# Pooled attention and two feed-forward layers on one core: attention and weight preparation moved to the one-product steps, squares on ScalarE, pools in the other order, 96 bytes added

## The chip, the cores and the metric

The kernel runs on one core of a Trainium2 chip. The metric is the time of one execution on the device in microseconds (us); the median of three runs of the kernel before is 1854.59 us.

## The reference

Three layers follow one another, all in float32:

```python
# 1: attention, B, H, S, D = 8, 8, 576, 64; keys and values averaged over groups of 8
k_p = k.reshape(B, H, 72, 8, D).mean(axis=3); v_p = v.reshape(B, H, 72, 8, D).mean(axis=3)
scores = np.matmul(q, k_p.transpose(0, 1, 3, 2)) / 8
attn = softmax(scores); x = np.matmul(attn, v_p)      # laid out as 4608 tokens x 512
# 2: 512 -> 2048 -> 512
h = x @ w_in; g = s * np.maximum(h, 0)**2 + b; x = g @ w_out
# 3: 512 -> 1536 -> 512
out = (sigmoid(x @ w_gate) * (x @ w_val)) @ w_out2
```

## The kernel before

Every operand of the large products is split into a high and a low part in the type float32r, and a product is three matmuls (low x high, high x high, high x low). Weights arrive as 64-bit words; `convert` makes float32 of them (one ScalarE and three VectorE instructions a tile) and `split` makes the two parts (ScalarE copies the high part, VectorE or GpSimd subtracts).

**First part** (layers 1 and 2). The tokens are 9 blocks of 512. A list of 176 slots sets the order: 16 slots for block 0, then for each of four pairs of blocks (p = 0 to 3) 40 slots x = 0 to 39. In a slot x < 32 the first product of layer 2 for one group of 128 hidden rows runs (`emit_h`, 12 matmuls of 512 columns; those of the next pair's x = 0 and 1 are put at x = 32 and 33 of this pair). Two slots later the second product of a chunk runs (`mm_chunk`). A pair's second product goes by a scheme with fewer multiplications: eight steps for each of z = 0 to 4. Steps with x < 24 (z = 0, 1, 2) have one product of 6 matmuls, steps of z = 3 and z = 4 two of them, 12 matmuls. So a one-product step holds 18 matmuls, a step of z = 3 has 24, a step of z = 4 has 12 and no `emit_h`. From slot 16 on TensorE's order is the order in which the program is written; the other engines' orders and the DMA queue of SyncE (SP) are set by a planner that simulates the program when it is built.

Beside the slots, at half-slot positions (`events`), runs the attention of layer 1: 18 units of 256 tokens (`scores`, `norm`, `left`, `turn`, `values`), units 0 and 1 ahead of the slots. A unit takes 13 positions, that is 6.5 slots. Keys and values of a batch are loaded up to 20 positions ahead and summed by GpSimd (`pool_k`, `pool_v`). `starts` holds the units' first positions: 0, 16, 32, 48, 64, 80 for units 2 to 7, then 80 p + 16, 40, 64, 80. A slot x of pair p is position 32 + 80 p + 2 x, so in p = 0 units start at x = 0, 8, 16, 24 and 32, in p = 1 and 2 at x = 4, 16, 24 and 32, and in p = 3 at x = 4.

`prep_w2` prepares layer 3's weights in 12 x 9 parts, one a slot, in slots 34 to 141. `prep_s` (layer 2's combined weights) stands at slots 14 to 45. `gen_x` prepares layer 3's first inputs `xo` beside slots 155 and 159.

**Second part** (layer 3). For each of four pairs and 12 groups `first_half` and `second_half` run seven `product`s of six matmuls (weights `w7` stationary, `xo` moving), `emit_o` the output product; the last block has 12 groups of four `product`s. 2,304 matmuls are `product`'s. `w1_stack.close()` ends the first part's pools, and `w7p`, `wo2p`, `g2p` and `wk` take their place; a tile of theirs waits for the tiles of the first part that lay there.

**Where the tiles lie.** Pools on the left side are stacked upwards in the order of their definition: constants, `gp`, `cvp`, then `w1_stack`: `wr_p` (12 KB a partition), `gs_p` (34), `us_p` (8), `gr_p` (2), `rawp` (12), `wi_p` (12), `xp` (32). `w7p` (two tiles of 14 KB) therefore lies on `wr_p` and eight tiles of `gs_p`. Attention's pools lie on the right side, and later `xop` with `xo`. In the allocation of the program before, every left tile that TensorE reads in the second part begins at a multiple of 256 bytes, `xo` begins at 172,000, which is 224 above a multiple of 256, 96 above a multiple of 128 and 32 above a multiple of 64; attention's operands `v1h`, `v1l`, `v3`, `t1` to `t3` on the right have the same remainders as `xo`. Between the last byte of the left side and the first of the right side 96 bytes are free in the first part.

Of the kernel before, what the change touches and what calls it, by code (L numbers as in the profile page):

```python
# [8 lines left out]
F32 = mybir.dt.float32  # L9
F32R = mybir.dt.float32r  # L10
I32 = mybir.dt.int32
ACTF = mybir.ActivationFunctionType
ALU = mybir.AluOpType
# [6 lines left out]
def pooled_attention_two_ffn(ctx, tc, q, k, v, v_left, w_in, w_out, s_in, b_in, w_gate, w_val, w_out2, out):  # L20
# [8 lines left out]
    nc = tc.nc  # L29
    NT, DM = out.shape  # L30
    NU, _, NP, UNIT = q.shape
# [3 lines left out]
    H = 2 * NP  # L35
    KD = DM // 128
    M1 = w_in.shape[0]
    M2 = w_gate.shape[0]
    NB = NT // 512

    const = ctx.enter_context(tc.tile_pool(name="const", bufs=1))
# [7 lines left out]
    ident = const.tile([128, 128], F32, name="ident")  # L49
    s_sb = const.tile([128, 1], F32, name="s_sb")  # L50
    b_sb = const.tile([128, 1], F32, name="b_sb")

    def split(hi, lo, src, eng):

        nc.scalar.activation(out=hi, in_=src, func=ACTF.Copy)  # L55
        eng.tensor_tensor(out=lo, in0=src, in1=hi.bitcast(F32), op=ALU.subtract)  # L56
# [3 lines left out]
    NB1 = NBLK // 2  # L60
    H1 = M1 // 2
# [7 lines left out]
    def load64(src):  # L69
        raw = rawp.tile([128, 1024], I32, tag="raw", name="raw")  # L70
        nc.sync.dma_start(out=raw, in_=src.bitcast(I32))
        return raw

    def cv_tile():
        return cvp.tile([128, 512], I32, tag="cv", name="cv")
# [19 lines left out]


    w1_stack = ExitStack()
    wr_p = w1_stack.enter_context(tc.tile_pool(name="wr_p", bufs=3))
    gs_p = w1_stack.enter_context(tc.tile_pool(name="gs_p", bufs=17))
    us_p = w1_stack.enter_context(tc.tile_pool(name="us_p", bufs=1))  # L100
    gr_p = w1_stack.enter_context(tc.tile_pool(name="gr_p", bufs=1))
    rawp = w1_stack.enter_context(tc.tile_pool(name="rawp", bufs=3))
    wi_p = w1_stack.enter_context(tc.tile_pool(name="wi_p", bufs=3))
    xp = w1_stack.enter_context(tc.tile_pool(name="xp", bufs=2))
    at_stack = ExitStack()
    at1 = at_stack.enter_context(tc.tile_pool(name="at1", bufs=1, side="right"))
    at2 = at_stack.enter_context(tc.tile_pool(name="at2", bufs=2, side="right"))
# [53 lines left out]
    def gs_tile():  # L161
        return gs_p.tile([128, 512], F32, tag="gs", name="gs")
# [56 lines left out]
    def store_split(dst, raw, src):  # L219
        n = src.shape[1]  # L220
        t = raw.rearrange("p (two f) -> p two f", two=2)[:, :, :n]
        split(t[:, 0].bitcast(F32R), t[:, 1].bitcast(F32R), src, nc.gpsimd)
        later.append((dst, t))

    def raw_tile():
        return rawp.tile([128, 1024], I32, tag="raw", name="raw")

    def prep_w2(m, part):
        h0, h1 = slice(0, 256), slice(256, 512)
        if part == 0:  # L230
            prep["g"] = load64(w_gate[m])
        elif part == 1:
            prep["v"] = load64(w_val[m])
        elif part == 2:
            raw = prep["g"]
            prep["gt"] = convert(raw, cv_tile())
            store_split(w7d[m][:, :, 256:768], raw, prep["gt"])
        elif part == 3:
            prep["vt"] = convert(prep["v"], cv_tile())
            store_split(w7d[m][:, :, 0:256], raw_tile(), prep["vt"][:, h0])  # L240
        elif part == 4:
            gt, vt, c = prep["gt"], prep["vt"], cv_tile().bitcast(F32)
            for o, a, b_, op in ((c[:, h1], gt[:, h0], vt[:, h0], ALU.subtract), (vt[:, h0], vt[:, h0], vt[:, h1], ALU.add),
                                 (c[:, h0], vt[:, h0], gt[:, h0], ALU.subtract), (gt[:, h1], gt[:, h1], c[:, h0], ALU.subtract)):
                nc.gpsimd.tensor_tensor(out=o, in0=a, in1=b_, op=op)
            prep["c"] = c
        elif part == 5:
            store_split(w7d[m][:, :, 768:1280], prep["v"], prep["vt"])
        elif part == 6:
            store_split(w7d[m][:, :, 1280:1792], raw_tile(), prep["c"])  # L250
        elif part == 7:
            store_split(w7d[m][:, :, 1792:2048], raw_tile(), prep["gt"][:, h1])
            prep["o"] = load64(w_out2[m])
        else:
            store_split(wo2d[m], prep["o"], convert(prep["o"], cv_tile()))
# [3 lines left out]
    def emit_h(i):  # L259
        j, m = steps[i]  # L260
        n = blocks[j][1]
        hi, lo = wi.pop(i)
        ps = ps_b.tile([128, 512], F32, tag="b", name="hps")[:, :n]
        a, c = x_tiles(j)
        step = UNIT if i < 2 else n
        for t0 in range(0, n, step):
            f = slice(t0, t0 + step)
            for kk in range(KD):
                nc.tensor.matmul(out=ps[:, f], lhsT=hi[:, kk], rhs=c[:, kk, f], start=kk == 0, stop=False)  # L269
                nc.tensor.matmul(out=ps[:, f], lhsT=hi[:, kk], rhs=a[:, kk, f], start=False, stop=False)  # L270
                nc.tensor.matmul(out=ps[:, f], lhsT=lo[:, kk], rhs=a[:, kk, f], start=False, stop=kk == KD - 1)  # L271
        first = j % 2
        if j and m < H1:
            g = gs_tile()
        else:
            g = gp.tile([128, 512], F32, tag="g", name="g", bufs=3)
        nc.scalar.activation(out=g, in_=ps, func=ACTF.Relu)
        if first:
            nc.vector.tensor_tensor(out=g, in0=g, in1=g, op=ALU.mult)
        else:  # L280
            nc.scalar.activation(out=g, in_=g, func=ACTF.Square)
        if j == 0:
            nc.scalar.activation(out=g, in_=g, func=ACTF.Identity, scale=s_sb, bias=b_sb)
        g_t[j, m] = g
# [304 lines left out]
    def left(u, t):  # L589
        pm, pl = e_t[u, t]  # L590
        lt = at2.tile([128, H, 4, 8], F32R, tag="lt", name="lt")
        for sl in (0, 2):
            nc.scalar.activation(out=lt[:, :, sl], in_=pl, func=ACTF.Copy)
        for sl in (1, 3):
            nc.vector.tensor_tensor(out=lt[:, :, sl], in0=pl, in1=lt[:, :, sl - 1].bitcast(F32), op=ALU.subtract)
        e_t[u, t] = pm, lt

    def turn(u, t, part):
# [44 lines left out]
    def at(pos, fn, *args):  # L643
        events.setdefault(pos, []).append((fn, args))

    starts = [16 * (u - 2) for u in range(2, 8)]
    for p in range(1, NB1):
        starts += [80 * p + x for x in (16, 40, 64, 80)]
    starts = dict(enumerate(starts, 2))
    for b in range(1, B):  # L650
        p = starts[b * S // UNIT]
        at(max(p - 20, 0), load_kv, b, "k")
# [8 lines left out]
    for u in range(2, NU):  # L661
        p = starts[u] + (2 if u == 2 else 0)
# [70 lines left out]
    if True:  # L733
# [61 lines left out]
        chunks = [(None, i) for i in range(M1)] + [(p, x) for p in range(NB1) for x in range(5 * H1)]  # L795
        hidden, used = {}, []
        for slot, (p, x) in enumerate(chunks):
# [4 lines left out]
            if p is None or x >= 3 * H1 or x % 2:  # L802
                used.append((slot + LAG, p, x))
        asked = M1

        def mm(slot):
            p, x = chunks[slot]
# [6 lines left out]
        for slot, (p, x) in enumerate(chunks):  # L814
            i = hidden.get(slot)
            swap = p is not None and x == 4 * H1 + 1
            if slot == M1:
                pe_order.enter_context(tc.manual_schedule(engines={mybir.EngineType.PE}))
            store_later()
            for fn, args in events.pop(2 * slot, []):  # L820
                fn(*args)
            if i is not None:
                load_wi(i + 3)
                if not swap:
                    emit_h(i)
            if 34 <= slot < 34 + 9 * M2:
                prep_w2(*divmod(slot - 34, 9))
            if M1 - 2 <= slot < 2 * M1 - 2:
                prep_s(*divmod(slot - M1 + 2, 2))
            if slot == 2 * M1:  # L830
                prep_bias()
            if p is None:
                split_wi(i + 2)
                split_g(i)
                split_wo(i + 1)
                load_wo(i + 2)
            else:
                prep_chunk(p, x, 0)
            for fn, args in events.pop(2 * slot + 1, []):
                fn(*args)  # L840
            if slot >= LAG:
                mm(slot - LAG)
            if p is not None:
                prep_chunk(p, x, 1)
            if swap and i is not None:
                emit_h(i)
            while asked < len(used) and used[asked - 3][0] <= slot:
                _, p1, x1 = used[asked]
                fetch_s(p1, x1 - (x1 < 3 * H1))
                asked += 1  # L850
            if p is not None and 3 * H1 - 2 <= x < 4 * H1 - 2:
                reload(p, x - 3 * H1 + 2)
            if i == NS - M1:
                assert not any(y < 2 * len(chunks) for y in events), events
                at_stack.close()
                xop = ctx.enter_context(tc.tile_pool(name="xop", bufs=1, side="right", reuse_waits="tile"))
            if i in (NS - M1 + 3, NS - M1 + 7):
                gen_x(0, (i - NS + M1) // 7)
# [180 lines left out]
```

## Time and profile before

| | |
|---|---|
| median of three runs | 1854.59 us (1852.23 to 1854.65) |
| the profiled execution | 1852.05 us, its span 1850.3 us |
| busy share of the span | TensorE 94%, VectorE 61%, ScalarE 39%, GpSimd 24% |
| mean granted TensorE clock | 0.969 of full speed |
| ahead of block 0's first `emit_x` matmul | 0 to 81.2 us |
| block 0 | 81.2 to 207.5 us |
| pairs p = 0 to 3 | 207.5 to 1011.0 us |
| second part | 1011.0 to 1850.3 us |

The span is that of the profiled execution, 1.75 us shorter than its time. Busy times of engines overlap. A stage of the first part is given by the first matmuls of its `mm_chunk`s: pairs p = 0 to 3 begin at 207.5, 431.7, 637.4 and 839.6 us, their z = 3 at 338.1, 545.6, 751.9 and 943.8, their z = 4 at 389.5, 598.4, 803.9 and 979.2. PEclk is the share of full speed that TensorE was granted, 1 for 2.4 GHz and 0.5 for 1.2 GHz at any moment.

### The profile page before, as it was taken

To read this page: it belongs to the slowest core of one execution; us is meant where nothing else is said; L and a number is where in the kernel's file an instruction comes from. 1 tells how busy PE (TensorE), PEld (TensorE's weight loads), DVE (VectorE), ACT (ScalarE), POOL (GpSimd) and SP (SyncE) were. 2 spreads that over 40 slices of the span, in tenths; PEclk is the share of its full clock that TensorE was granted. 3 is DMA by queue.
4 is the path that set the end of the run, shared out by engine and by line. 5 is a ranking of instruction groups with operands and counts; after the bars stand their busy time and mean duration, and the time that the engine had idled before them with its cause. 6 is when DMAs were issued, how large, how long until landed. Compare 5 with 4: busy or idle time off the path is not lost.

```text
span 1850.3 us, 22182 instructions
## 1 busy us (share of the span) xinstructions
PE 1736.1 (94%) x7848; PEld 1422.2 (77%) x7848; DVE 1124.4 (61%) x1736; ACT 721.1 (39%) x1303; POOL 436.0 (24%) x447
## 2 busy tenths in 40 slices
PE   4688899979999899989997999999999999999999
PEld 4566687768877788778886888888888888888887
DVE  7999766878678786875474544554445544454111
ACT  2556545545555555554454222222222222222111
POOL 5788605444252363321000000000000000000000
PEclk7788999989999899999998999999999999999999
DMA  7667998969897889867877555855585558554764
GB/s 273 237 196 243 350 315 267 324 238 329 302 329 271 253 332 351 304 222 235 257 221 256 184 172 200 284 188 183 187 284 190 198 173 286 194 193 169 264 228 141
DMA packets 159550, 454.46 MB, mean 246 GB/s; under 512 B 15696, under 2 KB 37200, under 8 KB 159440
## 3 DMA queue, kind: packets, MB, share of 16 engines
q1 hardware_dynamic: 155920, 441.51, 69.4%
q0 software_dynamic: 3520, 11.54, 1.9%
q8 instruction: 62, 1.02, 0.2%
q14 instruction: 48, 0.39, 0.1%
HBM read 371.20 MB, written 81.79 MB: 245 GB/s over the span
## 4 chain that ended last, share of the span: by engine, by line
PE 68%; DVE 13%; DMA 7%; POOL 4%; issue 4%; ACT 2%; SPq 0%; POOLq 0%; ACTq 0%; DVEq 0%
PE pc L887 5%; PE pc L885 5%; PE pc L886 5%; PE acc L942 5%; PE acc L941 5%; PE acc L943 5%; PE pb L885 4%; PE pb L886 4%; PE pb L887 4%; PE hps L269 4%; PE hps L271 4%; PE hps L270 4%; PE acc L374 3%; PE acc L376 3%; PE acc L375 3%
## 5 line engine op out<-in xcount | busy, mean ns | idle before, releaser
L891 DVE TENSOR_TENSOR wk<-pc,wk 128x512 f32<-128x512 f32 x192 | 132.5, 690 | 249.5 <-PE pc L887 247.6
L269 PE MATMUL hps<-xl,wi 128*128 128x512 f32 (+1 forms) x584 | 238.3, 408 | 13.0 <-DVE xl L56 5.8
L271 PE MATMUL hps<-xh,wi 128*128 128x512 f32 (+1 forms) x584 | 233.1, 399 | 0.0
L270 PE MATMUL hps<-xh,wi 128*128 128x512 f32 (+1 forms) x584 | 232.0, 397 | 0.0
L753 POOL DMA_DIRECT2D cv<-x2d x36 | 19.5, 542 | 712.1 <-DMA out<-eo 621.2
L374 PE MATMUL acc<-gl,wr 128*128 128x512 f32 x448 | 179.3, 400 | 2.6 <-DVE gl L56 2.1
L375 PE MATMUL acc<-gh,wr 128*128 128x512 f32 x448 | 177.0, 395 | 0.0
L376 PE MATMUL acc<-gh,wr 128*128 128x512 f32 x448 | 176.9, 395 | 0.0
L902 ACT ACTIVATE g<-pb 128x512 f32<-128x512 f32 x60 | 35.9, 598 | 361.9 <-PE pb L887 361.9
L886 PE MATMUL pc<-xo,w 128*128 128x512 f32 x432 | 170.9, 396 | 0.0
L887 PE MATMUL pc<-xo,w 128*128 128x512 f32 x432 | 170.9, 396 | 0.0
L885 PE MATMUL pc<-xo,w 128*128 128x512 f32 x432 | 170.9, 395 | 0.0
L55 ACT ACTIVATE gh<-g 128x512 fp32r<-128x512 f32 x140 | 87.8, 627 | 168.2 <-DVE g L903 144.3
L56 DVE TENSOR_TENSOR gl<-gs,gh 128x512 fp32r<-128x512 f32 x160 | 125.7, 790 | 32.4 <-ACT gh L55 30.1
L885 PE MATMUL pb<-xo,w 128*128 128x512 f32 x336 | 133.9, 398 | 9.3 <-DMA w<-w7d 9.3
L269 PEld LDWEIGHTS hps<-xl,wi 128*128 128x128 f32 x584 | 114.0, 195 | 35.9 <-DVE xl L56 6.0
L55 ACT ACTIVATE gh<-gs 128x512 fp32r<-128x512 f32 x160 | 100.3, 629 | 88.7 <-DVE gs L300 41.0
L886 PE MATMUL pb<-xo,w 128*128 128x512 f32 x336 | 133.6, 398 | 0.0
L887 PE MATMUL pb<-xo,w 128*128 128x512 f32 x336 | 133.4, 397 | 0.0
L271 PEld LDWEIGHTS hps<-xh,wi 128*128 128x128 f32 x584 | 114.2, 196 | 24.2
L270 PEld LDWEIGHTS hps<-xh,wi 128*128 128x128 f32 x584 | 114.1, 195 | 21.4
L56 POOL TENSOR_TENSOR raw<-cv,raw 128x512 fp32r<-128x512 f32 (+1 forms) x72 | 95.6, 1334 | 147.1 <-ACT raw L55 128.7
(143 smaller groups left out, 3713.3 us busy)
## 6 DMA issues: line engine op xcount, KB each, us to landing
w<-w7d SPq DMA_DIRECT2D x48, 1792.0 KB, 7.6
wi<-w1d SPq DMA_DIRECT2D x128, 512.0 KB, 5.3
wr<-s1d SPq DMA_DIRECT2D x224, 256.0 KB, 4.5
wo<-wo2d SPq DMA_DIRECT2D x108, 512.0 KB, 4.5
raw<-in SPq DMA_DIRECT2D x68, 512.0 KB, 5.5
w7d<-raw SPq DMA_DIRECT2D x36, 512.0 KB, 4.3
w<-w7d SPq DMA_DIRECT2D x12, 1280.0 KB, 6.5
kv<-in SPq DMA_DIRECT2D x24, 512.0 KB, 6.4
```

The source lines that it names most:

```text
L55: nc.scalar.activation(out=hi, in_=src, func=ACTF.Copy)
L56: eng.tensor_tensor(out=lo, in0=src, in1=hi.bitcast(F32), op=ALU.subtract)
L269: nc.tensor.matmul(out=ps[:, f], lhsT=hi[:, kk], rhs=c[:, kk, f], start=kk == 0, stop=False)
L270: nc.tensor.matmul(out=ps[:, f], lhsT=hi[:, kk], rhs=a[:, kk, f], start=False, stop=False)
L271: nc.tensor.matmul(out=ps[:, f], lhsT=lo[:, kk], rhs=a[:, kk, f], start=False, stop=kk == KD - 1)
L374: nc.tensor.matmul(out=a, lhsT=w[:, 0, f], rhs=gl, start=begin, stop=False, skip_group_check=True)
L375: nc.tensor.matmul(out=a, lhsT=w[:, 0, f], rhs=gh, start=False, stop=False, skip_group_check=True)
L376: nc.tensor.matmul(out=a, lhsT=w[:, 1, f], rhs=gh, start=False, stop=end, skip_group_check=True)
L885: nc.tensor.matmul(out=ps, lhsT=w[:, 0, x, kk], rhs=r[:, 1, kk, :n], start=first and kk == 0, stop=False, skip_group_check=True)
L886: nc.tensor.matmul(out=ps, lhsT=w[:, 0, x, kk], rhs=r[:, 0, kk, :n], start=False, stop=False, skip_group_check=True)
L887: nc.tensor.matmul(out=ps, lhsT=w[:, 1, x, kk], rhs=r[:, 0, kk, :n], start=False, stop=kk == 1, skip_group_check=True)
L891: nc.vector.tensor_tensor(out=o, in0=ps, in1=b_, op=ALU.add)
```

## The change

- `starts`: units 2 and 3 stay at 0 and 16; the others start at x = 0, 6, 12 and 18 of each pair, so that they lie in slots x < 24.5.
- `prep_w2`: its 108 parts go to the slots from 34 on with x < 32 (without every fourth of p = 1's z = 3), the last one being slot 167. None stands beside z = 4.
- `emit_h`: the square of blocks 1, 3, 5 and 7 (64 instructions) is made by ScalarE instead of VectorE.
- `left`: two ScalarE and two VectorE instructions of 64 elements become one and one of 128.
- `w1_stack`: its pools are defined in the other order, `xp` first and `wr_p` last, so that `w7p` and `wo2p` lie on `xp` and `wi_p`.
- A constant of 96 bytes a partition is added, which nothing reads. All pools on the left side behind it move by 96 bytes.

```diff
+    const.tile([128, 24], F32, name="pad")
...
-    wr_p = w1_stack.enter_context(tc.tile_pool(name="wr_p", bufs=3))
-    gs_p = w1_stack.enter_context(tc.tile_pool(name="gs_p", bufs=17))
+    xp = w1_stack.enter_context(tc.tile_pool(name="xp", bufs=2))
+    wi_p = w1_stack.enter_context(tc.tile_pool(name="wi_p", bufs=3))
+    rawp = w1_stack.enter_context(tc.tile_pool(name="rawp", bufs=3))
     us_p = w1_stack.enter_context(tc.tile_pool(name="us_p", bufs=1))
     gr_p = w1_stack.enter_context(tc.tile_pool(name="gr_p", bufs=1))
-    rawp = w1_stack.enter_context(tc.tile_pool(name="rawp", bufs=3))
-    wi_p = w1_stack.enter_context(tc.tile_pool(name="wi_p", bufs=3))
-    xp = w1_stack.enter_context(tc.tile_pool(name="xp", bufs=2))
+    gs_p = w1_stack.enter_context(tc.tile_pool(name="gs_p", bufs=17))
+    wr_p = w1_stack.enter_context(tc.tile_pool(name="wr_p", bufs=3))
...
-        if first:
-            nc.vector.tensor_tensor(out=g, in0=g, in1=g, op=ALU.mult)
-        else:
-            nc.scalar.activation(out=g, in_=g, func=ACTF.Square)
+        nc.scalar.activation(out=g, in_=g, func=ACTF.Square)
...
-        for sl in (0, 2):
-            nc.scalar.activation(out=lt[:, :, sl], in_=pl, func=ACTF.Copy)
-        for sl in (1, 3):
-            nc.vector.tensor_tensor(out=lt[:, :, sl], in0=pl, in1=lt[:, :, sl - 1].bitcast(F32), op=ALU.subtract)
+        l4 = lt.rearrange("p h (c two) j -> p h c two j", two=2)
+        both = pl.unsqueeze(2).to_broadcast([128, H, 2, 8])
+        nc.scalar.activation(out=l4[:, :, :, 0], in_=both, func=ACTF.Copy)
+        nc.vector.tensor_tensor(out=l4[:, :, :, 1], in0=both, in1=l4[:, :, :, 0].bitcast(F32), op=ALU.subtract)
...
-    starts = [16 * (u - 2) for u in range(2, 8)]
-    for p in range(1, NB1):
-        starts += [80 * p + x for x in (16, 40, 64, 80)]
-    starts = dict(enumerate(starts, 2))
+    starts = [0, 16] + [2 * M1 + 80 * p + x for p in range(NB1) for x in (0, 12, 24, 36)]
+    starts = dict(enumerate(starts[:NU - 2], 2))
...
+        light = [slot for slot, (p, x) in enumerate(chunks) if slot >= 2 * M1 + 2 and x < 4 * H1 and (x < 3 * H1 or x % 4 or p != 1)]
+        parts = dict(zip(light, (divmod(i, 9) for i in range(9 * M2))))
...
-            if 34 <= slot < 34 + 9 * M2:
-                prep_w2(*divmod(slot - 34, 9))
+            if slot in parts:
+                prep_w2(*parts[slot])
```

## Rows read from the trace of the kernel before

**Rows 1.** Busy time by stretch: stretch, length, PE, PEld, DVE, ACT, POOL, PEclk, DMA, GB/s
```profile
81.20:207.50 126.30, 108.24 (x474) 87.13 (x475) 119.28 (x144) 74.70 (x140) 105.44 (x92) 0.91 0.73 241
207.50:256.60 49.10, 43.39 (x206) 36.12 (x206) 32.54 (x61) 22.19 (x44) 15.08 (x17) 0.93 1.02 373
...
338.10:389.50 51.40, 48.00 (x226) 39.83 (x224) 44.59 (x72) 26.86 (x52) 15.21 (x14) 0.97 0.80 280
389.50:431.70 42.20, 30.34 (x138) 24.44 (x138) 33.19 (x50) 19.25 (x37) 27.74 (x29) 0.88 0.80 266
431.70:471.30 39.60, 38.53 (x190) 31.91 (x189) 32.46 (x56) 24.79 (x47) 16.54 (x16) 1.00 0.99 350
471.30:506.00 34.70, 34.70 (x163) 28.99 (x162) 19.31 (x32) 15.45 (x27) 7.44 (x9) 1.00 0.85 275
...
545.60:598.40 52.80, 49.13 (x242) 40.25 (x240) 48.04 (x76) 24.98 (x49) 20.35 (x18) 1.00 0.83 298
598.40:637.40 39.00, 33.33 (x139) 26.51 (x139) 29.34 (x49) 19.78 (x36) 12.06 (x12) 0.87 0.75 250
...
713.50:751.90 38.40, 38.40 (x198) 32.01 (x197) 30.45 (x48) 25.13 (x48) 20.26 (x17) 1.00 0.85 301
751.90:803.90 52.00, 49.70 (x241) 41.46 (x240) 43.29 (x75) 26.89 (x53) 13.53 (x12) 0.97 0.81 279
803.90:839.60 35.70, 30.67 (x139) 25.27 (x138) 25.61 (x42) 17.91 (x34) 12.28 (x12) 0.90 0.70 229
...
877.70:910.30 32.60, 32.60 (x146) 26.99 (x145) 11.28 (x17) 12.33 (x20) 1.08 (x2) 1.00 0.80 248
...
943.80:979.20 35.40, 35.40 (x157) 29.29 (x157) 23.84 (x39) 16.90 (x29) 0.00 (x0) 1.00 0.65 209
```

**Rows 2.** Waits of TensorE over the span: total us, times, longest us
```profile
PE tm L611 <- POOL pm L586: 23.1, 7, 9.3
PE tl L617 <- DVE lt L595: 12.0, 8, 4.7
...
PE pb L885 <- DMA w<-w7d: 9.3, 1, 9.3
```

**Rows 3.** Timeline of SP's queue at the end of the first part
```profile
1001.77 21.47 SPq L876 DMA_DIRECT2D w<-w7d  x3
```

**Rows 4.** Timeline of TensorE, end of the first part and start of the second
```profile
994.78 0.39 PE L374 MATMUL acc<-gl,wr 128*128 128x512 f32 x1
...
1001.35 0.39 PE L376 MATMUL acc<-gh,wr 128*128 128x512 f32 x1
...
1012.04 0.63 PE L887 MATMUL pb<-xo,w 128*128 128x512 f32 x1
...
1013.32 0.63 PE L887 MATMUL pb<-xo,w 128*128 128x512 f32 x1
```

**Rows 5.** Timeline of TensorE: a run of 36 `product` matmuls and the matmul behind it
```profile
1104.81 0.40 PE L885 MATMUL pc<-xo,w 128*128 128x512 f32 x1
...
1113.21 0.39 PE L941 MATMUL acc<-wo,gl 128*128 128x512 f32 x1
```

**Rows 6.** Timeline of TensorE: first and last of eight matmuls of `values`
```profile
363.86 0.28 PE L629 MATMUL pv<-t,v1h 128*128 128x256 f32 x1
...
364.70 0.28 PE L632 MATMUL pv<-t,v 128*128 128x256 f32 x1
```

**Rows 7.** Groups by line and form: busy us, mean ns of one | idle before, releasers
```profile
L56 DVE TENSOR_TENSOR gl<-gs,gh 128x512 fp32r<-128x512 f32 x160 | 125.7, 790 | 32.4 <-ACT gh L55 30.1
...
L87 DVE SCALAR_TENSOR_TENSOR cv<-raw,cv 128x512 int32<-128x512 int32 x52 | 46.6, 900 | 0.3
...
L595 DVE TENSOR_TENSOR lt<-pl,lt 128x64 fp32r<-128x64 f32 x72 | 43.4, 638 | 11.6 <-ACT lt L593 11.6
...
L56 DVE TENSOR_TENSOR sl<-g,sh 128x512 fp32r<-128x512 f32 x48 | 32.7, 681 | 2.8 <-ACT sh L55 2.8
...
L281 ACT ACTIVATE g<-g 128x512 f32<-128x512 f32 x48 | 30.1, 628 | 0.9
...
L279 DVE TENSOR_TENSOR gs<-gs 128x512 f32<-128x512 f32 x32 | 24.8, 774 | 11.9 <-ACT gs L277 11.6
```

More of the change, by code (lines that the diff above doesn't have):

```diff
@@ L271, in emit_h @@
                 nc.tensor.matmul(out=ps[:, f], lhsT=lo[:, kk], rhs=a[:, kk, f], start=False, stop=kk == KD - 1)
-        first = j % 2
         if j and m < H1:
@@ L804, in pooled_attention_two_ffn @@
         asked = M1
+        light = [slot for slot, (p, x) in enumerate(chunks) if slot >= 2 * M1 + 2 and x < 4 * H1 and (x < 3 * H1 or x % 4 or p != 1)]
+        parts = dict(zip(light, (divmod(i, 9) for i in range(9 * M2))))
+        assert len(parts) == 9 * M2, len(parts)
         def mm(slot):
```

## The prediction, made before the change was run

> **What bounds the kernel now.** I read the stretches of the first part first [rows 1], because a busy share over the whole span mixes stages with different limits. The reader should look at two things in a row: how much of the stretch TensorE (PE) is not busy, and the granted clock. Their price is length minus PE busy, plus PE busy times (1 - PEclk); it is an upper price, since a slow clock while PE idles costs nothing.
>
> Where a stretch holds neither attention nor weight preparation the price is nothing: x = 8 to 15 of p = 3 (877.7 to 910.3 us) and z = 3 of p = 3 (943.8 to 979.2) have PE busy throughout at full clock [rows 1]. With them, z = 3 costs 3.4 + 1.4 in p = 0, 3.7 in p = 1 and 2.3 + 1.5 in p = 2, together 12.3 us; z = 4, which has only 12 matmuls a step, costs 11.9 + 3.6, 5.7 + 4.3 and 5.0 + 3.1, together 33.6 us [rows 1]. VectorE (DVE) is busy for 72 to 91% of these six stretches. So the six stages in which a unit of attention runs beside two-product steps lose 46 us. One-product stages lose little: 1.1 us in x = 0 to 7 of p = 1, nothing in x = 8 to 15 of p = 1 and in x = 16 to 23 of p = 2, the last with DVE busy for 79% [rows 1]; the eleven of them behind the first have 6 us together, by the same reckoning. The first (207.5 to 256.6 us) loses 5.7 + 3.0 with the DMA engines full.
>
> Next I read PE's waits. The largest are of the transposes for attention: on GpSimd's `pm`, seven times, 9.3 us the longest, and on DVE's `lt` [rows 2]. One single wait of 9.3 us stands apart: the second part's first matmul waits for the weights `w7`. SP issues that load at 1001.77 us [rows 3], just behind the last matmul of the first part at 1001.35 [rows 4]: `w7` lies on `wr_p`, which that matmul still reads.
>
> Last, in the second part, the starts of matmuls. 36 `product` matmuls take 8.40 us, 233.3 ns each [rows 5]. The 30 of `mm_chunk` from 994.78 to 1001.35 have 29 distances, 226.6 ns each [rows 4]. Eight of `values`, with 256 columns, are 120 ns apart [rows 6]. From 256 to 512 columns is 106.6 ns, so a column takes 0.417 ns and what remains is 13.3 ns for `values` and `mm_chunk`, but 20 ns for `product`, of the same form. What sets it apart is where its operands lie: in `mm_chunk` both lie on the left side, in `values` both on the right, and in `product` the stationary on the left and the moving on the right, 32 bytes apart modulo 64.
>
> **The change part by part.**
>
> *Attention and weight preparation leave z = 4, attention leaves z = 3.* Without both, z = 3 and z = 4 should look like p = 3's; z = 3 keeps weight preparation. I leave 4 of the 46 us: -42. The bounds are 0 and 16 left (2.7 us in each stage, two thirds of what z = 3 loses now, would be as much).
>
> *They go to one-product steps.* DVE there: x = 0 to 15 of p = 1 are busy 32.5 + 19.3 = 51.8 us now with one unit [rows 1]. Twice the 11.3 us of the stretch without attention and preparation leaves 29.2. Preparation has nine conversion instructions in nine slots, at up to 0.90 us [rows 7], so 14.4 us in 16 slots, and a unit is 14.8 us. After: 16 squares leave DVE, 16 x 0.774 = 12.4 us [rows 7], and 1.67 more units come, 24.7: 64 us. PE's own time is 73.2 us plus 1.67 units; a unit's is 38.5 + 34.7 - 2 x 32.6 = 8.0 us, so 86.6 us. DVE is then busy for 74%, less than in x = 16 to 23 of p = 2, which loses nothing. ScalarE takes 16 squares of 0.628 us [rows 7], 10 us, on 40 now, and attention's share: about 60 of 87 us, so it hides. I take 1.1 us of loss for each of the eleven stages: 12 in place of 6, +6. The bounds are 0 and +22, 2 us more a stage: 2.3 to 3.7 us of idle time is what z = 3 has in 52 us with DVE at 83 to 91%. Preparation now lasts to slot 167, beside p = 3 and `gen_x`. They share the `cv` tiles, and SP's later loads of `raw` stand ahead of those of `wi` and `wr` in its queue. DVE has room there (11.3 of 32.6 us, 23.8 of 35.4 [rows 1]); I put nothing, and up to 5 us.
>
> *`left`.* Two DVE instructions of 0.638 us become one of twice the elements; between no dearer than 0.638 and the 0.774 of a 512-element one [rows 7], it saves 0.5 to 0.64 us a tile. Beyond the first stages it lies beside PE's work. In block 0 DVE is busy for 94% of the stretch [rows 1] and eight waits on `lt` sum to 12.0 us [rows 2]; eight tiles of units 0 to 3 are there, so 4 to 5 us at the most. I take -3, bounds 0 and -5.
>
> *Pools.* `w7` now lies on `xp`. Its last reader is the last `emit_h` at slot 167, and behind that come 8 steps of z = 4, 96 matmuls x 0.227 = 22 us; `wo2` lies on `xp` and `wi_p`, free at the same time. The load that took 9.3 us fits into 22. On SP it is queued with loads of `wr`, each of which waits for a step's matmuls, so it may go late by a step, 2.7 us. `wk` comes onto `wr_p` and the last four `gs`; the first four results of `first_half` need the latter. With the 9.3 us goes the slow clock behind the pause: matmuls stood 427 ns apart from 1012.04 to 1013.32 [rows 4], the 1.2 GHz level after 9.3 idle us; eight at 0.2 us make 1.6. I take -10.5, bounds -11 and -4.
>
> *96 bytes.* Left tiles move to 96 above a multiple of 128, as `xo` and attention's tiles are already. If the distance of a matmul's two operands makes the 6.7 ns, `product` falls to 226.6: 2,304 x 6.7 ns = -15.4. If not, 0. If instead only the moving operand's own start matters, all left/left matmuls pay: below. `values`, both operands 32 above a multiple of 64, paying 13.3 ns speaks for the distance. I take -15.4. What no row shows is whether 128 modulo 256 is near enough.
>
> Sum: -42 + 6 - 3 - 10.5 - 15.4 = -65 on the profiled 1852.05: **1787 us**. The three runs' median is 2.5 us higher, within their spread.
>
> **The rivals.**
>
> 1. *The pad does nothing.* For it: no row has operands 128 apart modulo 256. Then 1787 + 15 = 1802.
> 2. *The pad slows the others.* If the moving operand's own start costs the 6.7 ns, `product` stays and about 3,200 matmuls of 512 columns in the first part and 1,296 of `emit_o` get it: 4,500 x 6.7 ns = 30 us, so 1787 + 15 + 30 = 1832. Against it: `values` would show 127 ns, not 120 [rows 6].
> 3. *One-product steps fill up.* DVE's subtraction takes 0.790 us in the first part, 0.681 in the second, where GpSimd is idle [rows 7]. Packed closer to GpSimd's sums, DVE's 64 us could grow by as much again, 16%: 74 us of 87, 85%, and the stages lose like z = 3, 3.5 us each: 11 x 3.5 = 38 instead of 12. That is 1813. The Trainium skill has a rule that gives this: a VectorE instruction with two SBUF inputs and a GpSimd instruction that reads SBUF hold a port pair exclusively, the later one waiting for the whole of the earlier (SBUF — State Buffer, Who interferes with whom). By that rule the two durations differ by such waits, and the trace agrees in direction, at 109 ns an instruction.
> 4. *The other side: attention's chain waits in every tile.* PE's order is fixed, and `turn` waits for GpSimd's `pm`, queued behind sums and weight subtractions. Units now follow every six slots, 28 tiles from unit 4 on. Now seven waits average 3.3 us [rows 2]; were each of 28 tiles to pay it, 92 us, the time is 1879. From 65 / 28 = 2.3 us a tile on, the change loses. For it: the 9.3 us wait. Against it: that was in z = 4, where four positions are 5.4 us of matmuls; in one-product steps they are 8.2, and x = 16 to 23 of p = 2 has a unit and no idle time [rows 1].
> 5. *The change moves stalls to other places and gains nothing*, the planner giving SP or GpSimd an order with new waits worth 65 us: 1852.
>
> **How the numbers follow.** The forecast 0.52 (own range 1770 to 1798), the pad without effect 0.20, the pad slowing others 0.06, filled steps 0.12, tile waits 0.07, nothing gained 0.03. The lowest sum by the bounds is -46 - 5 - 11 - 15.4 = -77, 1775 us; block 0's stretch has 18 us of idle time besides [rows 1], and half of that could go with a new order: 1766. Upwards the range takes in the pad without effect together with half of the filled steps' 26 us and the 10 us by which preparation beside p = 3 (5) and `w7`'s load (6.5) may miss their values, some 1825. Above lie 0.06, 0.07 and 0.03. So 1766 to 1825. Faster by over 0.2% (3.7 us, about what a measurement can tell from no change) is 0.90, the same 0.03, slower 0.07.
>
> **What would show it.** In the profile after, PE should be busy to over 97% at full clock in z = 3 and z = 4 of p = 0 to 2; the waits on `pm` should not grow; `w7`'s load should be issued before the first part's last matmul, without a wait on it; `product` matmuls should stand 227 ns apart, `emit_o` and `mm_chunk` unchanged. Block 0 should change by a few us only. The prediction is wrong if `product` stays at 233 ns, if `mm_chunk` goes to 233, or if idle time of over 2 us a stage comes up in one-product steps.

## The result, and the profile after

The changed kernel takes 1872.2 us (median of four runs, 1870.4 to 1883.8) and the kernel before, beside it, 1853.8 (1852.2 to 1854.7): a ratio of 1.011, 95% interval 1.007 to 1.016. It is slower, where 1787 us was forecast. The profiled execution is the longest of the four, 1883.81 us with a span of 1882.0; a second trace, of 1871.5 us, has the same pauses at the same places.

First the busy time by stretch of the kernel after (columns as in [rows 1]): z = 3 and z = 4 of p = 0, the first 47 us of p = 1 (one-product steps), and z = 3 and z = 4 of p = 2 and of p = 3.

```profile
354.10:394.90 40.80, 40.80 (x181) 33.79 (x180) 27.22 (x44) 19.78 (x34) 0.00 (x0) 1.00 0.78 260
394.90:421.40 26.50, 26.50 (x126) 22.25 (x125) 16.68 (x31) 12.10 (x20) 3.42 (x6) 1.00 0.67 204
421.40:468.50 47.10, 37.45 (x168) 30.75 (x167) 28.98 (x48) 25.51 (x50) 28.43 (x28) 0.86 0.81 286
...
770.50:811.30 40.80, 40.80 (x182) 33.78 (x181) 26.34 (x43) 19.60 (x33) 0.00 (x0) 1.00 0.73 238
811.30:844.30 33.00, 29.63 (x126) 24.38 (x125) 18.49 (x34) 13.43 (x23) 9.42 (x9) 0.90 0.77 256
...
960.90:1022.10 61.20, 38.51 (x158) 30.75 (x156) 39.87 (x63) 26.74 (x49) 21.89 (x12) 0.86 0.76 273
1022.10:1045.60 23.50, 23.50 (x96) 19.31 (x97) 8.07 (x12) 6.95 (x11) 0.00 (x0) 0.92 0.51 169
```

The stages that were to be freed are free: z = 3 of p = 0 and p = 2 last 40.8 us with PE busy throughout at full clock, where [rows 1] has 51.4 and 52.0, and z = 4 of p = 0 lasts 26.5 in place of 42.2. Only z = 4 of p = 2 keeps 3.4 us of idle time, a wait on `wr`. But the first 47.1 us of p = 1, one-product steps, have PE idle for 9.65 us, and z = 3 of p = 3, which lost nothing before [rows 1], has 22.7 us of idle time, the last 13.3 of them at its end, so that z = 4 begins at a slow clock (0.92 over the stage). PE's waits over the span (total us, times, longest us) name what is behind it:

```profile
PE tm L608 <- POOL pm L583: 18.4, 6, 6.9
PE acc L371 <- DMA wr<-s1d: 16.7, 2, 13.3
...
PE sps L556 <- DVE e L564: 13.3, 5, 4.6
PE acc L371 <- DVE gl L57: 11.9, 5, 7.1
...
PE sps L556 <- DVE xl L57: 10.7, 7, 2.1
```

The wait on `pm` has shrunk a little [rows 2]. New in the pairs are waits of `scores` on `e` and `xl`, and one of 13.3 us on `wr`; the wait on `w7` is gone.

**An account by stages.** The loss of a stage is its length less its matmuls at their own full-clock distance (226.7 ns at 512 columns), so attention's matmuls may move without counting. The distance of attention's small matmuls is an estimate from these traces; another choice moves a row of the table by some 2 us. Against the profiled 1852.05 of before:

| term of the prediction | forecast | measured |
|---|---|---|
| z = 3 and z = 4 of p = 0 to 2 (49.3 us lost before, 6.7 after) | -42 | -42.6 |
| one-product stages (20.8 before, 80.3 after) | +6 | +59.5 |
| preparation beside z = 3 of p = 3 | 0 | +12.5 |
| boundary: z = 4 of p = 3 (10.0 to 1.8), and the new wait on `wr` | -10.5 (1.6 of it in the next row) | -8.2 + 13.3 |
| second part | -15.4 | -2.8 |
| ahead of the pairs (`left`) | -3 | +0.2 |
| sum | -65 | +31.9 (1883.81 - 1852.05 = 31.8) |

The second trace has 73.7 us of loss in one-product stages, 24.0 in place of 25.8 in z = 3 of p = 3, and 2.1 us less ahead of the pairs; that is most of the 12 us between the two executions. So the +59.5 above is +52.9 in the second trace, which is nearer to the other executions (1870.4 to 1872.8).

### The profile page after: what moved, and what is told of

Its sections match the earlier page's. It is cut to its first block, busy times and chain, and to the rows that moved or that the text cites. A ratio compares the mean times of both kernels' runs of the same rounds, so it can differ in the third digit from the quotient of the medians.

```text
span 1882.0 us, 22147 instructions
## 1 busy us (share of the span) xinstructions
PE 1744.7 (93%) x7848; PEld 1432.4 (76%) x7848; DVE 1061.8 (56%) x1636; ACT 751.6 (40%) x1331; POOL 428.5 (23%) x447
## 4 chain that ended last, share of the span: by engine, by line
PE 55%; DMA 3%; DVE 1%; POOL 1%; ACT 0%; issue 0%; SPq 0%; ACTq 0%; POOLq 0%
PE pc L885 5%; PE pc L884 5%; PE pc L883 5%; PE acc L940 5%; PE acc L941 5%; PE acc L939 5%; PE pb L885 4%; PE pb L883 4%; PE pb L884 4%; PE acc L371 2%; PE acc L372 2%; PE acc L373 2%; DMA wr<-s1d 2%; PE hps L270 2%; PE hps L271 2%; PE hps L272 1%
## 5 line engine op out<-in xcount | busy, mean ns | idle before, releaser
L271 PE MATMUL hps<-xh,wi 128*128 128x512 f32 (+1 forms) x584 | 235.6, 403 | 0.0
L272 PE MATMUL hps<-xh,wi 128*128 128x512 f32 (+1 forms) x584 | 235.1, 403 | 0.4 <-POOL wi L57 0.4
L57 DVE TENSOR_TENSOR gl<-g,gh 128x512 fp32r<-128x512 f32 x140 | 111.2, 794 | 62.2 <-ACT gh L56 57.4
L272 PEld LDWEIGHTS hps<-xh,wi 128*128 128x128 f32 x584 | 116.2, 199 | 25.3 <-POOL wi L57 0.8
L271 PEld LDWEIGHTS hps<-xh,wi 128*128 128x128 f32 x584 | 116.4, 199 | 21.6
L885 PE MATMUL pb<-xo,w 128*128 128x512 f32 x336 | 132.7, 395 | 0.0
L883 PE MATMUL pb<-xo,w 128*128 128x512 f32 x336 | 132.6, 395 | 0.0
```

Of the source, the lines that this page charges most:

```text
L883: nc.tensor.matmul(out=ps, lhsT=w[:, 0, x, kk], rhs=r[:, 1, kk, :n], start=first and kk == 0, stop=False, skip_group_check=True)
L885: nc.tensor.matmul(out=ps, lhsT=w[:, 1, x, kk], rhs=r[:, 0, kk, :n], start=False, stop=kk == 1, skip_group_check=True)
```

## The experiments

The experiments ran in four sets, each beside the kernel before on one chip (its medians are 1851.2 to 1853.1 us); ratios are to it. "Loss" is as above, from the experiment's trace.

**The changed kernel again.**

> The changed kernel once more, for a second trace. In the first trace its z = 3 of p = 3 lost 26 us, beginning with one GpSimd subtraction of 12.09 us (967.73 us) in front of which VectorE worked without a pause. If that stall belongs to the change's order, it is there again within 5 us; if it is a chance event of one execution, z = 3 of p = 3 loses under 15 us and the span is some 10 us shorter (1868 to 1872). In both cases the one-product stages should lose about 80 us again, the sum of z = 4 under 10 us, and the product matmuls stand 233 ns apart.

1871.5 us. The subtraction of 12.09 us is there again and z = 3 of p = 3 loses 24.0 us, so these pauses are the kernel's own. The 12 us by which this execution is shorter lie mostly in one-product stages.

**Which move costs: the old starts alone, the old preparation alone** (each the changed kernel with one edit).

```diff
 starts_before:
-    starts = [0, 16] + [2 * M1 + 80 * p + x for p in range(NB1) for x in (0, 12, 24, 36)]
-    starts = dict(enumerate(starts[:NU - 2], 2))
+    starts = [16 * (u - 2) for u in range(2, 8)]
+    for p in range(1, NB1):
+        starts += [80 * p + x for x in (16, 40, 64, 80)]
+    starts = dict(enumerate(starts, 2))
 w2_before:
-            if slot in parts:
-                prep_w2(*parts[slot])
+            if 34 <= slot < 34 + 9 * M2:
+                prep_w2(*divmod(slot - 34, 9))
```

> Attention's starts as before, all else as changed. Theory A (units that follow each other every 12 positions while each takes 13 make the new waits): the one-product stages fall from 80 to about 25 us of loss, z = 3 and z = 4 come back to a part of their old 59 us (30 to 50, weight preparation being away from z = 4), total 1835 to 1850. Theory B (weight preparation in the same steps and beside gen_x makes them): one-product loss stays above 60 us and the total above 1865. Theory C (the squares on ScalarE make them): as B.

> Weight preparation in slots 34 to 141 as before, all else as changed. Theory A: one-product loss stays at 70 to 85 us, z = 4 loses 5 to 15, z = 3 of p = 3 loses nothing since no preparation is left there: 1860 to 1875. Theory B: one-product loss falls below 40 us and the total below 1845.

1844.05 us (ratio 0.995, 0.994 to 0.997) and 1852.82 (1.000, 0.999 to 1.001). With the old starts the one-product stages lose 32.1 us, with the old preparation 57.7, against 80.3 and 73.7 in the two traces of the changed kernel. So the starts are what fills most of these stages with pauses, with the preparation adding to it. The old starts came out as theory A had it; with the old preparation both the loss and the time lie between the two theories. With the old preparation z = 3 of p = 3 loses 13.6 us, which is a wait on `wr` (the longest is 13.5): the other 12 belong to the preparation. Both traces also say something of the stages that were to be freed, z = 3 and z = 4 of p = 0 to 2, which lost 49.3 us before: with preparation away but attention left there they lose some 18 us, with attention away but preparation left there some 10. Either move alone frees most of them.

**What the scores wait for.** PE's timeline of the kernel after in x = 15 of p = 0 (start, length, line, operation, operands, idle time before it and its releaser):

```profile
301.78 0.28 PE L629 MATMUL pv<-t,v 128*128 128x64 f32 x1
301.89 0.74 PE L556 MATMUL sps<-kbd,qT 128*128 128x144 f32 x4
307.24 1.30 PE L556 MATMUL sps<-kbd,qT 128*128 128x144 f32 x4 [4.61 <-DVE e L564]
308.16 0.80 PE L270 MATMUL hps<-xl,wi 128*128 128x512 f32 x1
308.76 0.63 PE L271 MATMUL hps<-xh,wi 128*128 128x512 f32 x1
309.19 0.63 PE L272 MATMUL hps<-xh,wi 128*128 128x512 f32 x1
```

and VectorE's in the same stretch:

```profile
303.05 0.45 DVE L563 TENSOR_REDUCE mx<-sps 128x4 f32<-128x288 f32 x1
303.41 0.92 DVE L87 SCALAR_TENSOR_TENSOR cv<-cv,raw 128x512 int32<-128x512 int32 x1
304.25 1.27 DVE L88 SCALAR_TENSOR_TENSOR cv<-raw,cv 128x512 int32<-128x512 int32 x1
305.45 1.28 DVE L57 TENSOR_TENSOR gl<-gs,gh 128x512 fp32r<-128x512 f32 x1
306.65 0.45 DVE L564 TENSOR_TENSOR e<-sps,mx 128x288 f32<-128x288 f32 x1
307.01 0.68 DVE L57 TENSOR_TENSOR xl<-pv,xh 128x512 fp32r<-128x512 f32 x1
```

A unit's `values` are at its positions 12 and 13, and units now start 12 positions apart. So the next unit's first scores come right behind the `values` of the last one. `pv`, `sps`, `tm` and `tl` share the two tiles of the PSUM pool `ps_c`: one holds `pv` until `xl` has been made of it, the other the first half of the scores until `e` has, and the second half has to wait for either. Meanwhile VectorE runs a conversion of weights and `gl` ahead of both, and two of these instructions take 1.27 and 1.28 us, where `xl` behind them takes 0.68. PE waits 4.61 us, and behind the wait its matmuls stand 430 ns apart, the level of 1.2 GHz. This comes ten times, at the meeting of units (1.24 to 4.61 us, 21.4 together). Counted by `mm_chunk`, which runs two slots behind the starts, that is in x = 3, 9 and 15 of the pairs. The old starts were 16 positions apart at the least.

The test puts the scores of these units into `ps_a` (four tiles), and nothing else. The rival was `pm` on GpSimd; a second kernel makes `pm` and `pl` on VectorE.

```diff
 scores_ps_a:
+        pool = pool or (u > 4 and u % 4 != 0)
         ps = (ps_a if pool else ps_c).tile([128, 4, SP], F32, ...)
 pm_dve:
-            nc.gpsimd.tensor_tensor(out=o, in0=e[:, :, j], in1=sm..., op=ALU.mult)
+            nc.vector.tensor_tensor(out=o, in0=e[:, :, j], in1=sm..., op=ALU.mult)
```

> The changed kernel with the scores of the units that start at x = 6, 12 and 18 written to the two PSUM banks of ps_a that one-product steps leave free, instead of ps_c. Theory A1 (two ps_c banks for the values of one unit and the scores of the next make the new waits): the ten waits of the scores (21 us) go with their slow clock, 25 to 35 us less than the changed kernel, 1836 to 1847. Theory A2 (GpSimd's queue in front of pm is what costs): the waits of the scores turn into later ones on pm, under 10 us of change, 1862 to 1872.

> The changed kernel with norm's two products (pl and pm) on VectorE instead of GpSimd. Theory A1: the waits on pm (11 us in one-product stages) go, the scores' waits stay or grow with VectorE's 36 x 1 us more: 1858 to 1872. Theory A2: one-product loss falls by 30 us or more, 1840 or less.

1838.29 us (0.993, 0.990 to 0.995), 34 us under the changed kernel, and 1870.8 (1.010, 1.008 to 1.013), no gain. The loss of one-product stages falls to 43.3 us with the scores in `ps_a`. In that trace the same scores, with the matmul behind them, are

```profile
303.76 1.14 PE L557 MATMUL sps<-kbd,qT 128*128 128x144 f32 x8
304.64 0.49 PE L270 MATMUL hps<-xl,wi 128*128 128x512 f32 x1
```

eight in one go, and no wait of `scores` of over 0.9 us remains in the pairs. With `pm` on VectorE PE waits for `pm` all the same:

```profile
PE tm L608 <- DVE pm L583: 14.9, 5, 4.2
```

**The pools.** The kernel before with the new order of pools and the 96 bytes, and the same with the first loads of `w7` and `wo2` put behind the last load of `wr` on SP.

```diff
 w7_after_wr (on pools_alone):
-        fetch_w7(0, 0)
-        fetch_w7(0, 1)
+        with tc.issue_after(last_wr):
+            fetch_w7(0, 0)
+            fetch_w7(0, 1)
...
-                fetch_wo((p, 0, m))
+                if p == 0 and m < 4:
+                    with tc.issue_after(last_wr):
+                        fetch_wo((p, 0, m))
+                else:
+                    fetch_wo((p, 0, m))
```

> The kernel before with only the pools in the other order and the 96 bytes. The wait of 9.3 us at the start of the second part goes, with the slow clock behind it: 1843 (10 to 11 us less than before) by all theories; product matmuls at 233 ns as in the changed kernel. If the new places make waits elsewhere, it gains less than 7 us.

> The kernel before with the pools in the other order and the 96 bytes, and with the first loads of w7 and wo2 queued on SP behind the last load of wr. Theory P (the other order of pools lets the planner put 5.8 MB of w7 and wo2 loads in front of wr's, which then land late): the wait of 12.7 us on wr in z = 4 of p = 3 goes, and w7 lands within 2 us of the end of the first part: 1840 to 1845, 8 to 12 us less than before. Rival (the places themselves, or the DMA engines' load there, make the wait): the time stays at 1850 to 1856.

The first takes 1852.56 us (1.000, 0.999 to 1.002), a miss of 10 us; the second 1840.02 (0.994, 0.992 to 0.996). In SP's queue of the first (start, length of the issue, operands, count)

```profile
973.00 1.23 SPq L877 DMA_DIRECT2D w<-w7d  x2
974.28 2.68 SPq L881 DMA_DIRECT2D wo<-wo2d  x4
977.06 9.11 SPq L317 DMA_DIRECT2D wr<-s1d  x4
```

six loads of the second part, 2 x 1792 and 4 x 512 KB, 5.8 MB, stand ahead of the `wr` that PE needs next. From 977 to 994 us the DMA engines are busy throughout at 384 GB/s; 5.8 MB take 15 us of that, and PE's next matmul of the second product is

```profile
993.83 0.76 PE L375 MATMUL acc<-gl,wr 128*128 128x512 f32 x1 [12.74 <-DMA wr<-s1d]
```

Freed early, `w7` no longer waits; it now goes first, and `wr` waits. SP's queue of the second kernel:

```profile
969.74 20.44 SPq L317 DMA_DIRECT2D wr<-s1d  x16
990.24 1.23 SPq L878 DMA_DIRECT2D w<-w7d  x2
```

With the order put right z = 4 of p = 3 loses 1.9 us and its z = 3 nothing.

**The distance of the operands.** The kernel before with 224 unread bytes ahead of `xo` on the right side, so that `xo` and `w7` both begin at a multiple of 256; the order of all engines is that of before.

```diff
+                gap_p = ctx.enter_context(tc.tile_pool(name="gap_p", bufs=1, side="right", reuse_waits="tile"))
+                gap_p.tile([128, 56], F32, name="gap")
                 xop = ...
```

> The kernel before with 224 unread bytes ahead of xo on the right side, so that xo begins at a multiple of 256 bytes like the left tiles; the order of every engine is that of the kernel before. If the place of xo makes the 6.7 ns of a product matmul, the distance falls from 233.4 to 227 ns and the time by 15 us to 1837. If it has nothing to do with it, 233 ns and 1852.

1837.22 us (0.993, 0.990 to 0.995). First of a run of 42 `product` matmuls and the matmul behind it, in the kernel after (distance 128 modulo 256),

```profile
1111.14 0.40 PE L883 MATMUL pb<-xo,w 128*128 128x512 f32 x1
...
1120.93 0.39 PE L939 MATMUL acc<-wo,gl 128*128 128x512 f32 x1
```

and with `xo` moved (distance 0):

```profile
1112.94 0.39 PE L887 MATMUL pb<-xo,w 128*128 128x512 f32 x1
...
1122.46 0.39 PE L943 MATMUL acc<-wo,gl 128*128 128x512 f32 x1
```

9.79 / 42 = 233.1 ns and 9.52 / 42 = 226.7 ns a matmul. That is the 233.3 ns of [rows 5] at distances of 224 and of 128, and the 226.6 of `mm_chunk` [rows 4] at 0. 2,304 x 6.7 ns = 15.4 us by the 233.3 ns; the run gained 14.0.

**The mends together.** Three mends in the changed kernel: scores in `ps_a`, the loads behind `wr`, and 128 unread bytes ahead of `xo`, which puts `xo` and `w7` both at 96 above a multiple of 256. The fourth takes the preparation away from p = 3 from x = 16 on, where `gen_x` runs, and puts its 16 parts into z = 4 of p = 0 and 1. Then the squares are put back on VectorE, and in another kernel the old starts are taken (its scores stay in `ps_c`, where units 16 positions apart do not meet).

```diff
 four_fixes (three_fixes has the other edits, shown above):
-        light = [... if slot >= 2 * M1 + 2 and x < 4 * H1 and (x < 3 * H1 or x % 4 or p != 1)]
+        light = [... if slot >= 2 * M1 + 2 and (p < 2 or x < 4 * H1)
+                 and (x < 3 * H1 or x >= 4 * H1 or x % 4 or p != 1) and (p < 3 or x < 2 * H1)]
```

> The changed kernel with three things mended at once: scores of later units in the other two PSUM banks, the first loads of the second part's weights queued behind the last load of wr, and 128 unread bytes ahead of xo, so that xo and w7 both start 96 bytes above a multiple of 256 and lie at a distance of 0 modulo 256. If the distance of a matmul's two operands sets the pitch of product, it is 227 ns and the time 1838 - 12 - 14 = 1812 us. If the moving operand's own start sets it (xo no longer at a multiple of 256, as it was in the run at 227), product stays at 233 ns and the time is 1826. If the fixes lean on one another, more than 1830.

> The kernel with the three mends, and no weight preparation beside p = 3 from x = 16 on, where GpSimd makes xo: 16 of the 108 parts go to z = 4 of p = 0 and 1 instead. If the preparation beside p = 3 is what holds GpSimd's subtraction there (12.09 us) and SP's queue behind it, z = 3 of p = 3 loses its 12 us no more and z = 4 of two pairs loses some 2 us again: 10 us under the kernel with three mends, 1800 to 1803. If that subtraction would have been covered anyway, no difference, 1812.

> The kernel with four mends, the squares of blocks 1, 3, 5 and 7 back on VectorE. If VectorE's room decides in the one-product steps, 0.77 us more a step shows as 10 us or more of idle TensorE. If only waits on single tiles decide, within 4 us of the kernel with four mends.

> The kernel with four mends, but with attention's starts as they were before (and its scores in the old banks): is moving attention worth anything once the banks are mended? If z = 3 and z = 4 still lose there what they lost with attention (36 + 8 us in the kernel that has only the old starts, of which 12 are p = 3's), this is 10 us or more slower than four mends. If one-product steps give it back, the same within 4 us: 1844 - 12 - 14 - 12 = 1806.

| kernel | us | ratio | loss: one-product, z = 3, z = 4 |
|---|---|---|---|
| three mends | 1816.36 | 0.981 (0.980 to 0.983) | 42.2, 13.1, 9.4 |
| four mends | 1795.51 | 0.970 (0.968 to 0.972) | 33.7, 0, 7.0 |
| the same, squares on VectorE | 1800.36 | 0.972 (0.971 to 0.974) | 42.5, 0, 7.4 |
| the same as four mends, old starts | 1823.32 | 0.985 (0.983 to 0.987) | 28.9, 9.7, 32.7 |

`product` is at 226.7 ns with three mends: the distance decides, not where the moving operand begins. The time with three mends is 4 us above the 1812 that the single gains gave. The fourth mend gains 21 us where 10 were expected; 13 are z = 3 of p = 3, which is at PE's pace again (busy time by stretch, four mends):

```profile
909.30:944.70 35.40, 35.40 (x158) 29.29 (x157) 23.83 (x39) 16.88 (x29) 0.00 (x0) 1.00 0.63 208
```

and 8.5 are one-product stages, whose share in the gain was not taken apart. The squares are worth 5 us for 64 x 0.774 = 50 us of VectorE's time, between the under 4 and the over 10 that the two theories had. The last kernel is 28 us slower than four mends, 17 above the 1806 of the case that the gain is given back. Its 16 parts of the preparation lie beside attention in z = 4, which loses 14.4 and 10.9 us in p = 0 and 1; it could not price the move of attention alone.

**Each move by itself, with three mends.**

The kernel with three mends with the old starts (the edit of `starts_before`; the scores then stay in `ps_c`), with the old preparation (that of `w2_before`), and with both.

> The kernel with three mends, attention's starts as before (the scores then stay in the old banks), weight preparation as in the change. If moving attention out of z = 3 and z = 4 is worth something by itself once the banks are mended, this is 10 us or more slower than the kernel with three mends (1816), 1826 or more. If its gain there is given back in one-product steps, it is the run with only the old starts less the loads' order and the distance of the operands, 1844 - 12 - 14 = 1818, within 4 us of three mends.

> The kernel with three mends, weight preparation in slots 34 to 141 as before, attention's new starts. If moving the preparation is worth something (z = 4 freed of it), this is slower than the kernel with four mends (1795.5) by 10 us or more. If the preparation is harmless in z = 4 as soon as attention is gone from there, it is the run that has only the old preparation less the mends, 1853 - 34 - 11 - 14 = 1794, the same as four mends.

> The kernel with three mends and neither move: what is left of the change are the squares, left, the pools and the 96 bytes. By the sum of single runs 1840 (pools with the loads queued late) - 14 (operands at distance 0) = 1826, less up to 5 for the squares. Against four mends (1795.5) this prices the two moves together: 25 to 31 us if the freed stages count, under 10 if one-product steps give the gain back.

| | preparation in slots 34 to 141 | as in the change | away from p = 3, x >= 16 |
|---|---|---|---|
| old starts | 1820.07 | 1822.91 | 1823.32 |
| new starts | 1801.79 | 1816.36 | 1795.51 |

The ratios of the three new ones are 0.983 (0.981 to 0.985) for neither move, 0.984 (0.982 to 0.986) and 0.972 (0.970 to 0.974). With the banks mended, moving attention gains 18 us beside the old preparation and 6.5 beside the new. Moving the preparation as the change does loses 3 to 15 us; in its best place here it gains 6 with the new starts and loses 3 with the old. The two kernels with one move each fell between the cases set out for them (1822.9 between 1818 and 1826, 1801.8 between 1794 and 1805.5); the two moves together, in their best form, are worth 24.6 us, near the 25 of the case that the freed stages count.

## Why the prediction was wrong

*The step that failed is "+6" for one-product steps.* It measured 59.5, and 52.9 in the second trace. The work itself came about as reckoned. For p = 1, x = 0 to 15, the sum was 64 us of VectorE and 86.6 of PE; that stretch in the kernel after and, with the same matmuls, in the kernel with four mends (columns as in [rows 1]):

```profile
421.40:520.00 98.60, 86.06 (x421) 71.54 (x420) 59.32 (x100) 56.18 (x108) 46.50 (x49) 0.93 0.86 305
405.60:491.50 85.90, 82.76 (x421) 69.45 (x420) 58.81 (x100) 55.60 (x105) 40.34 (x44) 0.98 0.91 326
```

VectorE has 59.3 us, below the sum. PE's 86.1 hold matmuls at the slow clock; at 0.98 the same matmuls keep it busy for 82.8, so the 86.6 were some 4 us too high. But 98.6 us went by, and the bounds (0 to 22) were drawn from VectorE's busy share. That share did not decide: with as much VectorE work the stretch takes 85.9 us once the mends are in, and squares back on VectorE cost 5 us. What decided is an order. Units 12 positions apart overlap by the two positions of `values`, and two banks had to hold the tiles of both. No row of before shows it, since no two units had come so close; the list of starts beside the positions of one unit does. `scores_ps_a` shows it with 34 us. Of the remaining excess (43.3 less 20.8), the 6.9 us on `pm` in p = 1 are one wait; with four mends the excess is 13 us, and what each us of that waits for was not settled. The base was short as well: the prediction priced these twelve stages before at 6 + 8.7 us and called the price an upper one, and by their matmuls' distances they lost 20.8.

*z = 3 and z = 4 freed, -42.* Right in mechanism, and the size came out at -42.6; by the measure of the account both ends of it were about 3 us short (46 reckoned to be lost against 49.3, 4 left against 6.7), so that it came this close is in part luck.

*Preparation beside p = 3, "nothing, and up to 5".* It took 12.5. GpSimd's timeline of the kernel after,

```profile
967.73 12.09 POOL L57 TENSOR_TENSOR raw<-cv,raw 128x512 fp32r<-128x512 f32 x1 [9.94 <-ACT raw L56]
```

SP's,

```profile
967.66 0.38 SPq L138 DMA_DIRECT2D wi<-w1d  x1
979.85 0.52 SPq L153 DMA_DIRECT2D w7d<-raw  x1
980.46 1.44 SPq L313 DMA_DIRECT2D wr<-s1d  x2
```

and the last of VectorE's nineteen instructions that stand 0.6 us apart from 967.14 us on:

```profile
976.17 1.29 DVE L297 TENSOR_TENSOR gs<-g,gs 128x512 f32<-128x512 f32 x2
977.38 0.68 DVE L88 SCALAR_TENSOR_TENSOR cv<-raw,cv 128x512 int32<-128x512 int32 x1
977.98 0.68 DVE L57 TENSOR_TENSOR xo<-cv,xo 128x512 fp32r<-128x512 f32 x1
```

The subtraction ends when VectorE has paused, SP's store of its result waits for it, and the loads of `wr` and `gr` behind that store come late, those of `wr` by 12 us. PE's next matmul needs a `gl` that VectorE makes behind `gr`: VectorE's first instruction that reads it, at 988.53 us, has waited 9.87 us for the load.

```profile
982.54 0.37 SPq L318 DMA_DIRECT2D gr<-b21d  x1
989.88 0.80 PE L371 MATMUL acc<-gl,wr 128*128 128x512 f32 x1 [7.07 <-DVE gl L57]
```

The forecast saw the queue ("SP's later loads of `raw` stand ahead") and looked for room on VectorE alone.

*Pools, -10.5.* The wait on `w7` went; a larger one on `wr` came. The forecast let `w7` be late by a step and did not ask what 5.8 MB ahead of `wr` does to `wr`; `w7_after_wr` shows the 11 us that the step had meant.

*96 bytes, -15.4.* Rival 1 held here: 128 modulo 256 is not near enough. The mechanism, the distance, was right, and at 0 the size too. Rival 2 did not occur: `mm_chunk` stays at 227 ns.

*`left`, -3.* +0.2 and, in the second trace, -1.9: nothing that can be told.

*The other rivals.* Rival 3 took the one-product steps for the place, rightly, and VectorE against GpSimd for the cause. Half of it came. In one-product stages the instructions that make `gl` take 87.6 us for 98 in the kernel after and 76.7 for 99 before, 894 against 775 ns; that is 15% more, about the 16% of the rival, though over the whole kernel the mean of [rows 7] hardly moves (794 against 790). But VectorE's time in p = 1, x = 0 to 15, was 59.3 us and not 74, and in `scores_ps_a`, where `gl` takes 910 ns in these stages, 37 of the 80.3 us of loss are gone all the same. The Trainium skill's rule cited there (SBUF — State Buffer, Who interferes with whom) calls the port pair that VectorE and GpSimd share an exclusive lock. The traces agree with it on GpSimd's side too, and there with a wait over eighteen instructions of VectorE, not one. Rival 4, waits on `pm` in every tile, did not occur: six waits, 18.4 us, and moving `pm` to VectorE gains nothing. Rival 5, stalls that only move, came nearest: the new losses, 59.5 + 12.5 + 13.3 = 85 us, ate up the gain. It had put them at 65 us and into the orders of SP and GpSimd, where the two smaller ones do lie. The way of the largest, two units on two PSUM tiles, no rival described. Two of the signs of being wrong that the prediction named came true: `product` stayed at 233 ns, and idle time of over 2 us came up in one-product stages.

## What to carry to other kernels

Before work is packed closer, list what each unit holds (PSUM tiles above all) from its first to its last position: where two units overlap, count the tiles of both against the pool, because engine shares will not show it. A transfer that is freed early takes its place in a queue, so ask at once what stands behind it and how many bytes that waits for. Mend the pauses first and then judge a move: the same move of attention lost 28 us before the mends and gained 6.5 behind them, beside the same preparation.

## What the runs showed of the hardware

- The pitch of 512-column `product` matmuls depends on the distance of the operands' first bytes modulo 256: 233.4 ns at 224, 233.1 at 128, 226.7 at 0, whether both begin at 0 or both at 96. Other distances were not tried, nor whether 256 is the number that counts.
- One subtraction on GpSimd took 12.09 us (one of the same shape, at 982.8 us in the trace of the kernel after, took 1.26), to the hundredth the same in six kernels, while VectorE ran two-input instructions without a break; it ended 1.2 us after the last of them. Shorter unbroken runs of VectorE give shorter waits by the same measure: in `w2_before` (806.63 us) the run lasts 2.38 us into GpSimd's subtraction, which takes 3.53, and in `mends_old_w2` (784.87 us) 3.58 us and 4.73. In each case the subtraction ends 1.15 to 1.16 us behind VectorE's last. The port is argued from this, not tested by itself; with no GpSimd work in that stretch (four mends) the loss is gone.
